# Three of five f32 table products moved from VectorE's queue to GpSimd's

## The chip, the cores and the metric

The kernel runs on one core of a Trainium2 chip. The metric is the device time of one execution in microseconds, and the time shown for the kernel before is the median of three runs: 236.66 us (236.27 to 236.88). The engines are named as in the profile: PE is TensorE, DVE is VectorE, ACT is ScalarE, POOL is GpSimd, SP is SyncE, which issues most of the DMAs. Each engine works through its own list of instructions in order; an instruction that waits for a semaphore holds up everything behind it on that engine.

## The reference

Two independent computations are set side by side in the output. The first is a linear attention over 2048 tokens and 16 heads of 28; the second is a long convolution of 2048 steps, with one kernel per channel that comes from a diagonal state space of 256 states for each of 448 channels.

```python
def _A_ref(x, wqkv, w_phi, wo):
    q, k, v = ...                                  # x @ wqkv, by heads
    phi_q = concat([softmax(q @ w_phi), softmax(-q @ w_phi)])
    phi_k = concat([softmax(k @ w_phi), softmax(-k @ w_phi)])
    kv = einsum("bhsf,bhsd->bhfd", phi_k, v); z = einsum("bhsf->bhf", phi_k)
    o = (phi_q @ kv) / (phi_q @ z + 1e-6)
    return o.reshape(B, S, D) @ wo

def _B_ref(u, A_re, A_im, B_re, B_im, C_re, C_im, log_dt, Dskip):
    dt = exp(log_dt)
    P = exp(dt * (A_re + 1j * A_im) * l)           # l = 0 .. 2047, rounded to bf16
    K = einsum("dn,dnl,dn->dl", C, P, dt * B).real
    y = irfft(rfft(u, padded) * rfft(K, padded))[:2048]
    return y + u * Dskip

return concat([_A_ref(...), _B_ref(...)], axis=-1)
```

## The kernel before

The exponentials P are not computed for each of the 2048 steps. Positions are written as sums of a few powers, and for each power k in `LOWP` = (128, 16, 8, 32, 64) (L344) a table `PW[k]` of the k-th power of every state's pole is made: a magnitude `amp[k]` (an exponential on ACT, f32, 896 columns), a cosine and a sine `cs[k]` (two activations on ACT, f32, 2 x 896 columns), and their product `PW[k]` (128 x 1792, bf16; for k = 128 an f32 `q128` that is squared for k = 256). The five products are the `mul` of L368, which goes through the helper `tt` (L177) and so runs on DVE:

```python
for k in LOWP:
    af(by_states(cs[k][:, 0, :]), from_states(bT), ACT.Sin, scale=float(k), bias=bias_hp)
    ...
    mul(PW[k] if k != 128 else q128, cs[k], amp[k].unsqueeze(1).to_broadcast([128, 2, NCOL]))
```

After that the kernel works on four groups of 112 channels. `tables(qt)` builds the two factor tables of group qt: `hi_tables` multiplies a start table step by step with `PW[16]`, `PW[32]`, `PW[64]` and `PW[128]` into `U_`, and `damp` and `far` build `W` from `PW[8]` and `PW[256]`. Both are chains of bf16 products and sums on DVE, with a few copies and squares on ACT. `build_k` contracts the two on PE. `signal_spectrum` transforms the input u on PE, and ACT copies each result out of PSUM into a tile `sg` (L419, L429), from where a DMA stores it. `key_side` and `query_side` are the attention; `kernel_spectrum` and `conv` are the spectral product and the inverse transform.

Nothing is scheduled at run time or by a planner at build time. The functions only record operations, and three lists written out in the file decide the rest: `ORDER` (L827) is the order in which all 1008 recorded operations are issued, and so the order of each engine's own list; `PLACES` (L865) is the address of every SBUF tile in one large buffer; `PICKS` (L885) says for operations that ACT or DVE could do which one does them. Waits are then put in by the framework, from what overlaps in memory.

Tiles share addresses where `PLACES` lets them, and three such overlaps touch this change. `cs[16]` lies on the bytes of two `sg` tiles; `cs[64]` lies on the bytes of another `sg` tile; the last part of `U_` of group 1 lies on the start of `cs[32]`. So ACT's first copy into the first of these `sg` tiles has to wait until the product for k = 16 has read `cs[16]`, ACT's next copy (into the `sg` on `cs[64]`) until the product for k = 64 has read it, and the copy that starts `U_` of group 1 (L545) until the product for k = 32 has. In the list of ACT these are three copies (L205 in the profile), in that order; in the list of DVE the products come in the order 16, 64, 32, with a cast between 64 and 32 that belongs to `PW[256]` (L375).

The other operations of DVE near them are, in this order: a subtraction for `q256` (f32), the three products and the cast, then two bf16 sums of `signal_spectrum` (`ab`, L414), a scaling in `damp` (L496, L208 in the profile) and the first product of `damp` (128 x 3136). The two sums wait for ACT's copies of `ur` (L413), the scaling and the product for the exponentials of `dampings` (L479), which ACT makes in between the copies into `sg`.

Of the kernel before, what the change touches and what calls it, by code (L numbers as in the profile page):

```python
# [12 lines left out]
ALU = mybir.AluOpType  # L13
# [11 lines left out]
NCOL = 4 * QC  # L25
# [94 lines left out]
def kernel(  # L120
# [17 lines left out]
    nc = tc.nc  # L138
# [11 lines left out]
    prog = Prog()  # L150

    def sb(shape, dtype=BF16):
        off = prog.place()
        size = int(np.prod(shape[1:])) * (4 if dtype == F32 else 2)
        v = sbuf[0:shape[0], off // 2:(off + size) // 2]
        if dtype == F32:
            v = v.bitcast(F32)
        names = "abcdefg"[:len(shape) - 1]
        if len(names) > 1:
            v = v.rearrange(f"p ({' '.join(names)}) -> p {' '.join(names)}",  # L160
                            **{n: s for n, s in zip(names[1:], shape[2:])})
        return v
# [13 lines left out]
    def tt(o, a, b, op):  # L176
        prog.add("V", lambda: nc.vector.tensor_tensor(out=o, in0=a, in1=b, op=op))  # L177

    def mul(o, a, b):
        tt(o, a, b, ALU.mult)  # L180
# [16 lines left out]
    def af(o, a, fn, **kw):  # L197
        prog.add("A", lambda: nc.scalar.activation(o, a, fn, **kw))  # L198
# [5 lines left out]
    def copy(o, a):  # L204
        either(lambda: nc.scalar.copy(o, a), lambda: nc.vector.tensor_copy(o, a))  # L205
# [64 lines left out]
    def load_u(b):  # L270
# [5 lines left out]
        out=ldt.rearrange("p (u j) -> p u j", u=2),  # L276
# [4 lines left out]
        out=raw["Are"].rearrange("p (u j) n -> p u (j n)", u=2),  # L281
# [32 lines left out]
    def from_states(bs):  # L314
        return view(psum[:, bs[0], 0:1], [512 * (bs[1] - bs[0]), 2], [56, 8], [1, 56])

    def by_states(v):
        return view(v, [56, 2], [112, 8], [1, 56])
# [26 lines left out]
    PW = {k: sb([128, 2, NCOL]) for k in (8, 16, 32, 64, 128, 256)}  # L345
    amp = {k: sb([128, NCOL], F32) for k in LOWP}
    cs = {k: sb([128, 2, NCOL], F32) for k in LOWP}
    q128, q256 = (sb([128, 2, NCOL], F32) for _ in range(2))
# [16 lines left out]
    for k in LOWP:  # L365
        af(by_states(cs[k][:, 0, :]), from_states(bT), ACT.Sin, scale=float(k), bias=bias_hp)
        af(by_states(cs[k][:, 1, :]), from_states(bT), ACT.Sin, scale=float(-k if k == 8 else k))
        mul(PW[k] if k != 128 else q128, cs[k], amp[k].unsqueeze(1).to_broadcast([128, 2, NCOL]))  # L368
        if k == 128:
            copy(PW[128], q128)  # L370
    s2 = sb([128, 2, NCOL], F32)
# [544 lines left out]
```

## Time and profile before

| | |
|---|---|
| median of three runs | 236.66 us (236.27 to 236.88) |
| profiled execution, whole | 235.22 us |
| its span (first to last instruction) | 233.5 us |
| busy: DVE / PE / ACT / POOL | 216.8 / 208.1 / 183.9 / 4.6 us |
| granted TensorE clock | 1.00 |

In the profile, a row of the timeline gives the start in us, the duration in us, the engine, the line, the operation, and the shapes as partitions x elements. A row of the chain of waits gives start, duration and what the chain ran through in that time. L177, L205, L198 and L208 are helper lines (a two-operand DVE operation, a copy, an activation, a scaling), so that rows are told apart by shape, start and neighbour rather than by line.

### The profile page before, as it was taken

The numbers are of one execution on the slowest core, as the hardware profiler recorded it, in microseconds if no ns is written. First come the engines' busy times: TensorE is split into PE (matmuls) and PEld (weight loads), VectorE is DVE, ScalarE is ACT, GpSimd is POOL, SyncE is SP. The second block draws the span as 40 slices with busy tenths as digits, with TensorE's granted clock in tenths as the row PEclk, the third lists the DMA queues.
The fourth block names the chain that finished last, engine by engine and source line by source line (L and its number), as shares of the span: only waits on it lengthen the run. The fifth ranks groups of instructions, "written<-read, shape, count | busy, mean of one in ns | idle before, by whom it ended". The sixth has DMA issues, their size and how long they took to land.

```text
span 233.5 us, 7103 instructions
## 1 busy us (share of the span) xinstructions
PE 208.1 (89%) x3044; PEld 152.8 (65%) x3044; DVE 216.8 (93%) x267; ACT 183.9 (79%) x321; POOL 4.6 (2%) x20
## 2 busy tenths in 40 slices
PE   1173899998999999999987999999999999999994
PEld 1161446564557655589765678885579968689993
DVE  1799999999999999989999979999999999999980
ACT  3999999999999999999998998698328451355331
POOL 4000000000000100000000000000000000000000
PEclk9999999999999999999999999999999999999999
DMA  5999910499239999826865899872696890489643
GB/s 154 237 218 272 151 37 1 167 150 235 71 59 190 147 176 257 152 71 155 206 156 144 99 255 225 226 114 61 70 368 131 199 277 10 63 185 242 121 100 81
DMA packets 81640, 36.40 MB, mean 156 GB/s; under 512 B 65480, under 2 KB 79688, under 8 KB 81224
## 3 DMA queue, kind: packets, MB, share of 16 engines
q1 hardware_dynamic: 81368, 35.71, 73.3%
q8 instruction: 24, 0.39, 0.7%
q10 hardware_dynamic: 240, 0.23, 0.3%
q14 instruction: 8, 0.07, 0.1%
HBM read 19.44 MB, written 8.62 MB: 120 GB/s over the span
## 4 chain that ended last, share of the span: by engine, by line
PE 51%; ACT 17%; DVE 13%; DMA 5%; issue 3%; SPq 0%; ACTq 0%
PE psum L220 51%; DVE sbuf L177 11%; ACT sbuf L198 8%; ACT sbuf L205 7%; DMA sbuf<-sbuf 3%; DMA sbuf<-KTd 2%; ACT L198 1%; DVE sbuf L205 1%; DVE sbuf L194 0%; ACT sbuf L211 0%; SPq L240 0%; DVE sbuf L212 0%; ACT sbuf L208 0%; DVE sbuf L208 0%; PE psum L230 0%
## 5 line engine op out<-in xcount | busy, mean ns | idle before, releaser
L220 PE MATMUL psum<-sbuf 128*128 128x112 bf16 (+9 forms) x3000 | 206.2, 252 | 21.4 <-ACT sbuf L205 7.8
L177 DVE TENSOR_TENSOR sbuf<-sbuf 128x896 bf16<-128x896 bf16 (+11 forms) x222 | 197.3, 956 | 7.2 <-ACT sbuf L198 4.3
L220 PEld LDWEIGHTS <-sbuf 128*128 128x128 bf16 (+3 forms) x3000 | 150.1, 114 | 75.3 <-issue 18.2
L205 ACT CAST sbuf<-psum 128x448 bf16<-128x448 f32 (+4 forms) x129 | 79.7, 672 | 38.0 <-PE psum L220 37.3
L198 ACT ACTIVATE sbuf<-psum 128x448 bf16<-128x448 f32 (+4 forms) x110 | 65.5, 721 | 0.5 <-PE psum L220 0.4
L211 ACT ACTIVATE sbuf<-sbuf 128x896 bf16<-128x896 bf16 x14 | 14.2, 1024 | 4.0 <-DVE sbuf L177 4.0
L198 ACT ACTIVATE sbuf<-psum,sbuf 128x896 f32<-128x896 f32 (+3 forms) x17 | 13.6, 835 | 0.0
L208 ACT ACTIVATE sbuf<-sbuf 128x896 bf16<-128x896 bf16 (+2 forms) x10 | 10.9, 1091 | 1.4 <-DVE sbuf L299 0.8
L198 ACT ACT_TABLE_LOAD x8 | 10.3, 1283 | 1.4 <-PEq L900 1.3
L205 ACT COPY sbuf<-sbuf 128x224 bf16<-128x224 bf16 (+2 forms) x18 | 8.9, 512 | 0.0
L205 DVE CAST sbuf<-psum 128x448 bf16<-128x448 f32 (+3 forms) x8 | 5.3, 690 | 2.3 <-PE psum L220 1.7
L215 POOL MEMSET sbuf<- 128x224 bf16 (+4 forms) x15 | 4.2, 314 | 153.3 <-PE psum L220 153.1
L205 ACT COPY sbuf<-psum 112x896 bf16<-112x896 bf16 (+2 forms) x13 | 6.8, 549 | 0.1
L177 DVE TENSOR_TENSOR sbuf<-psum,sbuf 128x448 bf16<-128x448 f32 (+3 forms) x12 | 5.1, 444 | 0.1
L194 DVE RECIPROCAL sbuf<-psum 128x64 bf16<-128x64 f32 x8 | 4.3, 546 | 0.4 <-ACT sbuf L198 0.3
L230 PEld LDWEIGHTS <-sbuf 112*112 112x112 bf16 (+1 forms) x44 | 3.1, 128 | 1.8 <-DVE sbuf L177 0.8
L230 PE MATMUL psum<-sbuf 112*112 112x112 bf16 (+1 forms) x44 | 3.6, 215 | 0.6 <-DVE sbuf L177 0.6
L212 DVE TENSOR_TENSOR sbuf<-sbuf 128x896 bf16<-128x896 bf16 (+1 forms) x3 | 3.3, 1087 | 0.0
L194 DVE RECIPROCAL sbuf<-sbuf 128x64 f32<-128x64 f32 x4 | 2.2, 545 | 0.0
L189 DVE SCALAR_TENSOR_TENSOR sbuf<-sbuf 128x64 f32<-128x64 f32 (+1 forms) x5 | 2.0, 393 | 0.0
L205 ACT CAST sbuf<-sbuf 128x1792 bf16<-128x1792 f32 x1 | 1.8, 1814 | 0.0
L208 DVE TENSOR_SCALAR sbuf<-sbuf 128x1568 bf16<-128x1568 bf16 (+1 forms) x3 | 1.6, 538 | 0.0
(8 smaller groups left out, 2.1 us busy)
## 6 DMA issues: line engine op xcount, KB each, us to landing
SUd<-sbuf SPq DMA_DIRECT2D x8, 448.0 KB
sbuf<-SCd SPq DMA_DIRECT2D x16, 224.0 KB
sbuf<-SUd SPq DMA_DIRECT2D x4, 896.0 KB
sbuf<-const SPq DMA_DIRECT2D x3, 1024.0 KB
sbuf<-const SPq DMA_DIRECT2D x8, 384.0 KB
sbuf<-in_B_u_dram SPq DMA_DIRECT2D x4, 448.0 KB
out_dram<-sbuf SPq DMA_DIRECT2D x4, 448.0 KB
out_dram<-sbuf SPq DMA_DIRECT2D x16, 112.0 KB
```

The lines of the kernel that those rows point to most:

```text
L177: prog.add("V", lambda: nc.vector.tensor_tensor(out=o, in0=a, in1=b, op=op))
L189: prog.add("V", lambda: nc.vector.scalar_tensor_tensor(out=o, in0=a, scalar=s, in1=b, op0=op0, op1=op1))
L194: nc.vector.reciprocal(o, a)
L198: prog.add("A", lambda: nc.scalar.activation(o, a, fn, **kw))
L205: either(lambda: nc.scalar.copy(o, a), lambda: nc.vector.tensor_copy(o, a))
L208: either(lambda: nc.scalar.activation(o, a, ACT.Copy, scale=s), lambda: nc.vector.tensor_scalar_mul(o, a, s))
L211: either(lambda: nc.scalar.activation(o, a, ACT.Square), lambda: nc.vector.tensor_tensor(out=o, in0=a, in1=a, op=ALU.mult))
L212: lambda: nc.vector.tensor_tensor(out=o, in0=a, in1=a, op=ALU.mult))
L215: prog.add("G", lambda: nc.gpsimd.memset(o, v))
L220: nc.tensor.matmul(o, lhsT=l, rhs=r, **kw)
L230: nc.tensor.transpose(o, i, idn)
```

## The change

In the kernel after, the products for k = 16, 32 and 64 are recorded for GpSimd and issued as its `tensor_tensor`, with the same operands and data types; those for k = 128 and 8 stay on DVE. They are no longer recorded through `mul`, so their line in the profile is L369. `ORDER`, `PLACES` and `PICKS` are unchanged, and with them the position of the products in the order of issue.

```diff
     for k in LOWP:
         af(by_states(cs[k][:, 0, :]), from_states(bT), ACT.Sin, scale=float(k), bias=bias_hp)
         af(by_states(cs[k][:, 1, :]), from_states(bT), ACT.Sin, scale=float(-k if k == 8 else k))
-        mul(PW[k] if k != 128 else q128, cs[k], amp[k].unsqueeze(1).to_broadcast([128, 2, NCOL]))
+        on_pool = k in (16, 32, 64)
+        prog.add("G" if on_pool else "V", lambda k=k, e=nc.gpsimd if on_pool else nc.vector: e.tensor_tensor(
+            out=PW[k] if k != 128 else q128, in0=cs[k], in1=amp[k].unsqueeze(1).to_broadcast([128, 2, NCOL]), op=ALU.mult))
         if k == 128:
             copy(PW[128], q128)
```

In the engines' lists this takes three rows out of DVE's and puts three next to each other into POOL's, in the order 16, 64, 32, behind five memsets and ahead of a 64 x 448 memset for a weight tile. The first of them waits for the cosine of k = 16 (ACT) and for what lay in its output's place before; the other two have their inputs by then. The three copies on ACT that waited for DVE's products now wait for POOL's: the one into the `sg` on `cs[16]` for the first product, the one into the `sg` on `cs[64]` for the second, the one that starts `U_` of group 1 for the third. On DVE one later subtraction of `hi_tables` waits for POOL's third product. All other waits that change on PE and SP are for POOL's later memsets and for DMAs that are issued tens of microseconds on.

## The prediction

> **What bounds the kernel now.** I read the busy times first, then the busy time by stretch of the span, then the chain of waits, then the timelines of DVE and ACT around the products.
>
> ```profile
> span 233.5 us, 7103 instructions
> PE 208.1 (89%) x3044; PEld 152.8 (65%) x3044; DVE 216.8 (93%) x267; ACT 183.9 (79%) x321; POOL 4.6 (2%) x20
> ```
> ```profile
> 26.30:37.00 10.70, 9.75 (x50) 4.84 (x49) 10.70 (x10) 10.67 (x18) 0.00 (x0) 1.00 0.30 57
> 37.00:50.00 13.00, 12.84 (x98) 7.65 (x96) 13.00 (x20) 12.86 (x17) 0.00 (x0) 1.00 0.55 123
> 50.00:93.60 43.60, 41.45 (x483) 24.88 (x481) 43.02 (x51) 43.47 (x86) 1.07 (x4) 1.00 0.83 159
> 93.60:129.70 36.10, 32.43 (x601) 25.73 (x600) 35.09 (x62) 35.05 (x66) 0.51 (x2) 1.00 0.65 143
> 129.70:230.10 100.40, 100.36 (x1742) 81.30 (x1741) 95.38 (x107) 58.89 (x111) 0.51 (x2) 1.00 0.77 162
> ```
> The columns of the second fence are the stretch and its length, then the busy time of PE, weight loads, DVE, ACT and POOL. DVE has the most work and POOL almost none, which speaks for moving work. But by stretch three engines are full at once. Between 26.3 and 50 us DVE is busy for all of the time and ACT for all but 0.17 us; from 50 to 93.6 ACT has 0.13 us left; from 129.7 to 230.1 it is PE. Time taken off DVE alone in the second stretch is worth only what ACT can follow.
>
> ```profile
> 32.62 3.91 DVE sbuf L177 x3
> 36.52 0.53 DVE sbuf L208
> 37.05 4.42 DVE sbuf L177 x5
> ...
> 48.50 0.20 ACT sbuf L208
> ...
> 93.61 6.15 DMA sbuf<-sbuf
> ...
> 129.69 31.20 PE psum L220 x553
> ```
> The chain that ends last runs over DVE to 48.5 us, over ACT to 93.6, over a transposing DMA and PE, and from 129.7 on over PE alone. So a delay of DVE or ACT near 37 us has nothing behind it that would take it in: the later links depend on it one after the other, and what ACT could make up is 0.14 us in 37 to 50.
>
> **DVE loses three products.** Here is DVE before, row by row: a bf16 sum, the f32 subtraction, the products for k = 16 and 64, the cast, the product for k = 32, two bf16 sums of the input's spectrum, the scaling, the first product of `damp`.
>
> ```profile
> 25.56 1.09 DVE L177 TENSOR_TENSOR sbuf<-sbuf 128x1792 bf16<-128x1792 bf16 x1
> 26.56 1.08 DVE L177 TENSOR_TENSOR sbuf<-sbuf 128x896 f32<-128x896 f32 x1
> 27.56 2.02 DVE L177 TENSOR_TENSOR sbuf<-sbuf 128x1792 bf16<-128x1792 f32 x1
> 29.50 2.02 DVE L177 TENSOR_TENSOR sbuf<-sbuf 128x1792 bf16<-128x1792 f32 x1
> 31.43 1.18 DVE L205 CAST sbuf<-sbuf 128x1792 bf16<-128x1792 f32 x1
> 32.51 2.01 DVE L177 TENSOR_TENSOR sbuf<-sbuf 128x1792 bf16<-128x1792 f32 x1
> 34.44 1.08 DVE L177 TENSOR_TENSOR sbuf<-sbuf 128x1792 bf16<-128x1792 bf16 x1
> 35.44 1.08 DVE L177 TENSOR_TENSOR sbuf<-sbuf 128x1792 bf16<-128x1792 bf16 x1
> 36.44 0.61 DVE L208 TENSOR_SCALAR sbuf<-sbuf 128x1568 bf16<-128x1568 bf16 x1
> 36.98 1.77 DVE L177 TENSOR_TENSOR sbuf<-sbuf 128x3136 bf16<-128x3136 bf16 x1
> ```
> 2.02 + 2.02 + 2.01 = 6.05 us go. What is late next is ACT:
>
> ```profile
> 25.10 1.18 ACT L198 ACTIVATE sbuf<-psum,sbuf 128x896 f32<-128x896 f32 x1
> 29.53 0.92 ACT L205 CAST sbuf<-psum 128x896 bf16<-128x896 f32 x1
> 30.76 0.94 ACT L205 CAST sbuf<-psum 128x896 bf16<-128x896 f32 x1
> 31.80 0.96 ACT L205 CAST sbuf<-psum 128x896 bf16<-128x896 f32 x1
> 34.18 0.65 ACT L198 ACTIVATE sbuf<-psum 128x448 bf16<-128x448 f32 x1
> 35.40 1.05 ACT L198 ACTIVATE sbuf<-psum 128x896 bf16<-128x896 f32 x1
> 36.99 0.70 ACT L205 COPY sbuf<-sbuf 128x448 bf16<-128x448 bf16 x1
> ```
> The two sums need the copy of `ur` that ends at 29.53 + 0.92 = 30.45; the scaling needs the exponential that ends at 34.83; the 128 x 3136 product needs the one that ends at 35.40 + 1.05 = 36.45. DVE began that product at 36.98. So even free products would bring DVE forward by 36.98 - 36.45 = 0.53 us and no more; the other 5.5 us become idle time in front of ACT. And since ACT is full itself, of the 0.53 us only the 0.14 us of its own idle time in 37 to 50 can reach the end. The gain is at most 0.1 to 0.5 us.
>
> **POOL gains three products.** Their price is not in the trace, since POOL does no two-operand work before. The rows of POOL by shape and window, the two memset rows from the start and from 77 us on:
>
> ```profile
> L279 POOL TENSOR_SCALAR_AFFINE_SELECT sbuf<-sbuf 112x112 bf16<-112x112 bf16 x1 | 0.3, 281 | 0.1
> L215 POOL MEMSET sbuf<- 64x448 bf16 x2 | 0.9, 465 | 0.0
> L215 POOL MEMSET sbuf<- 128x128 bf16 x1 | 0.2, 198 | 0.0
> ...
> L215 POOL MEMSET sbuf<- 64x448 bf16 x1 | 0.5, 465 | 0.0
> ```
> A memset writes one stream: (465 - 198) / (448 - 128) = 0.834 ns per element beside 91 ns fixed. The affine select reads one and writes one: (281 - 91) / 112 = 1.70 ns per element. For 1792 elements that is 1792 x 1.70 + 91 = 3.13 us if a second operand is free, and 1792 x 3 x 0.834 + 91 = 4.57 us if it costs a third stream. Below, the price of one stream, 1.59 us, is a floor; above, 4.57 is my ceiling. The affine select is the nearest row, and a product does more than it, so I take the middle of the two, 3.85 us, an estimate. The Trainium skill, GPSIMD Engine Reference, section Performance versus the Vector engine, states 4497 ns for such an f32 operation over 2048 elements, which would be 3.94 us here, an estimate from that page; the sum below would grow by 0.3 us with it.
>
> **The waits that move with them.** The first product needs the cosine that ends at 26.28 and can start at about 26.3. On ACT the copy at 30.76 now waits for product one, the copy at 31.80 for product two, the one at 36.99 for product three, and each holds all of ACT's list behind it, the exponentials for DVE among it. With nothing else in the way: product one ends at 30.2 (in time), product two at 26.35 + 2 x 3.85 = 34.05, product three at 37.9. ACT's second copy is then 34.05 - 31.80 = 2.25 us late, and its third copy, due at 36.99 + 2.25 = 39.2, is not held further. The 128 x 3136 product starts at 36.45 + 2.25 = 38.7 instead of 36.98. Less the 0.14 us, that is 2.1 us at the end. POOL's memset of a weight tile, now behind the products, comes at 38 to 43 us instead of about 3; its first reader is a multiplication in the key side, after 57 us, so it costs nothing. The one wait of DVE for product three stands behind the 128 x 3136 product and is met by then. The DMAs whose waits name POOL now are issued later still.
>
> **Do the two engines work beside each other?** The second unknown is whether POOL's reading runs freely beside DVE.
>
> ```profile
> 77.40 2.79 DVE L177 TENSOR_TENSOR sbuf<-sbuf 128x3136 bf16<-128x3136 bf16 x2 [0.38 <-ACT sbuf L205]
> ```
> ```profile
> 77.49 1.07 POOL L215 MEMSET sbuf<- 128x224 bf16 x4 [74.32 <-PE psum L220]
> ```
> Beside a busy DVE POOL only ever writes here: the 64 x 448 memset takes 465 ns in that place as it does at the start, before DVE's first work. The affine select, the only row that reads, ran with DVE idle. So the trace bounds it from both sides: no cost (2.1 us, above), or full exclusion, in which DVE's operations with operands in SBUF and POOL's products take turns. Then this holds for the stretch from 26.56 to the scaling: three products, the f32 subtraction, the cast and two bf16 sums, one after the other, 3 x 3.85 + 1.08 + 1.18 + 2 x 1.08 = 16.0 us, so that the scaling starts at 42.5 instead of 36.44, 6.1 us late. If DVE goes first whenever it can, product one waits for the cast (28.7), product two ends at about 38.4, ACT's second copy is 6.6 us late and the 128 x 3136 product starts at 36.45 + 6.6 = 43.1: again 6.1 us. The order of turns hardly matters, since both engines' work must fit in before the same point. With 3.13 and 4.57 us per product it is 3.9 and 8.3 us.
>
> I take exclusion as the likelier: no row supports the free case, as POOL has never read beside DVE here, and both stream f32 operands from the same 128 partitions. That is a judgement, not a reading. The Trainium skill, SBUF — State Buffer, section Who interferes with whom, states it as a rule: a VectorE instruction with two SBUF inputs and a GpSimd instruction that reads SBUF hold each other off for the whole instruction. No run here shows it; by that rule the sum is the 6.1 us.
>
> **The sum.** 0 to 0.5 us gained, 6.1 us lost, net 6.1, as the gain is inside the serial sum already. Against the profiled execution that is 235.22 + 6.1 = 241.3 us. That execution was 1.44 us below the median of the runs, 236.66, and the forecast is for a median: 242.8 us.
>
> **The rivals.**
> - POOL runs freely beside DVE, and only ACT's wait for product two costs: 236.66 + 2.1 = 238.8 us (237.4 at 3.13 us per product, 240.3 at 4.57). For it: the memset row. Against it: a memset reads nothing.
> - Not slower: the products hide under ACT. The point from which this decides is the copy at 31.80: two products must end by then, so one may take (31.80 - 26.35) / 2 = 2.7 us, with no interference. DVE's own 2.02 us would do. Then the time is 236.66 less 0.1 to 0.5, about 236.4 us. Against it: at 1.70 ns per element the affine select gives 3.13 us.
> - Worse than the sum: products over 4.57 us each, or DVE's operations themselves stretched; beyond 245 us.
> - That the products stay on DVE is excluded by the lists of the engines: they lose and gain exactly these three rows.
>
> **How the numbers follow.** Exclusion 0.50, free running 0.33, not slower 0.12, worse 0.05. The predicted time is that of the first, 242.8 us. The range from 237.4 (free running with the cheapest product) to 245.0 (exclusion with the dearest) leaves out 0.12 and 0.05; the forecast's own range is 240.6 to 245.0. About 0.3%, 0.7 us, is what a measurement of this kernel can tell from no change: faster by more 0.02, within it 0.10, slower 0.88.
>
> **What would show it.** Right: POOL has three L369 rows between 26 and 43 us, at 3.1 to 4.6 us each when alone; ACT's idle time before L205 copies is released by POOL; DVE idles, or its rows there get longer, and the 128 x 3136 product begins near 43 us; from there the timeline is the old one, shifted. If the product begins near 38.7 with DVE's rows at their old durations, the engines ran freely. Wrong: products under 2.7 us, a DVE that runs past ACT, or a shift at 43 us that is gone by 130.

## The result

The kernel after takes 244.17 us (median of 4 runs, 243.16 to 244.84) against 236.47 us for the kernel before in the same comparison (4 runs, 234.77 to 236.88): the ratio is 1.034, with a 95% interval of 1.027 to 1.040. It is slower by 7.7 us. The profiled execution took 244.84 us, beside 235.22 us before. The ratios here and below compare fast runs with fast runs and leave slow ones out, so that a ratio need not be the quotient of the medians beside it.

From the page of the kernel after, the span, the busy times, the granted clock of TensorE by slices of 6.1 us (in tenths; 9 stands for full speed) and the group of the three products (busy time and mean ns of one, then the idle time ahead):

```profile
span 243.1 us, 7104 instructions
PE 212.5 (87%) x3044; PEld 154.9 (64%) x3044; DVE 222.5 (92%) x264; ACT 184.4 (76%) x321; POOL 18.3 (8%) x23
PEclk9999997699999999999998899999999999999999
...
L369 POOL TENSOR_TENSOR sbuf<-sbuf 128x1792 bf16<-128x1792 f32 x3 | 13.7, 4598 | 23.5 <-PE psum L220 23.5
```

DVE has three instructions fewer and is busy 222.5 us instead of 216.8: it lost 6.05 us of products and gained 5.7 us of busy time. POOL's three rows last 4.6 us in the mean; how much of that is work shows when the two engines are read side by side. The timelines of POOL and of DVE of the kernel after (start, duration), around the products:

```profile
26.26 4.11 POOL L369 TENSOR_TENSOR sbuf<-sbuf 128x1792 bf16<-128x1792 f32 x1 [23.50 <-PE psum L220]
30.33 4.82 POOL L369 TENSOR_TENSOR sbuf<-sbuf 128x1792 bf16<-128x1792 f32 x1
35.10 4.87 POOL L369 TENSOR_TENSOR sbuf<-sbuf 128x1792 bf16<-128x1792 f32 x1
```
```profile
25.45 1.08 DVE L177 TENSOR_TENSOR sbuf<-sbuf 128x1792 bf16<-128x1792 bf16 x1
26.45 4.86 DVE L177 TENSOR_TENSOR sbuf<-sbuf 128x896 f32<-128x896 f32 x1
31.35 4.83 DVE L205 CAST sbuf<-sbuf 128x1792 bf16<-128x1792 f32 x1
36.07 4.85 DVE L177 TENSOR_TENSOR sbuf<-sbuf 128x1792 bf16<-128x1792 bf16 x1
40.84 1.08 DVE L177 TENSOR_TENSOR sbuf<-sbuf 128x1792 bf16<-128x1792 bf16 x1
41.84 0.61 DVE L208 TENSOR_SCALAR sbuf<-sbuf 128x1568 bf16<-128x1568 bf16 x1
42.38 1.77 DVE L177 TENSOR_TENSOR sbuf<-sbuf 128x3136 bf16<-128x3136 bf16 x1
```

The subtraction takes 4.86 us instead of 1.08, the cast 4.83 instead of 1.18, the first bf16 sum 4.85 instead of 1.08; the second sum, issued when POOL has ended, takes 1.08 as before. Read the ends of the rows, since a held instruction counts as busy: the sum of DVE ends at 26.53, product one at 30.37 (3.84 later), the subtraction at 31.31 (0.94), product two at 35.15 (3.84), the cast at 36.18 (1.03), product three at 39.97 (3.79), the first sum at 40.92 (0.95). One engine works at a time, and they alternate strictly. The scaling starts at 41.84 instead of 36.44, 5.4 us late.

ACT and PE behind it, in the timelines of the kernel after:

```profile
35.18 0.91 ACT L205 CAST sbuf<-psum 128x896 bf16<-128x896 f32 x1 [3.33 <-POOL sbuf L369]
42.00 0.56 ACT L205 COPY sbuf<-sbuf 128x448 bf16<-128x448 bf16 x1 [1.43 <-issue]
```
```profile
40.98 3.17 PE L220 MATMUL psum<-sbuf 128*128 128x448 bf16 x8 [3.17 <-DVE sbuf L177]
43.94 1.70 PE L230 MATMUL psum<-sbuf 112*112 112x112 bf16 x16
```
```profile
40.00:46.00 6.00, 5.03 (x26) 3.05 (x27) 6.00 (x6) 2.99 (x4) 0.38 (x1) 0.51 0.01 1
```

ACT's copy waits 3.33 us for product two. PE waits 3.17 us for DVE's first bf16 sum, and from then on its granted clock is 0.51 (the last fence: PE, weight loads, DVE, ACT, POOL, clock, DMA share and GB/s in 40 to 46 us): the 7 and the 6 in the slices of the page. The chain of waits of the kernel after has PE in it here, and is otherwise the old one, later:

```profile
31.35 0.06 DVE sbuf L205
...
36.07 4.86 DVE sbuf L177
...
40.98 3.17 PE psum L220 x8
...
101.23 6.15 DMA sbuf<-sbuf
...
139.33 31.18 PE psum L220 x534
```

The transposing DMA at 93.61 us before stands at 101.23, 7.62 us later; the last long link, on PE, at 139.33 instead of 129.69, 9.64 us later. So of the 9.62 us between the two profiled executions 7.6 are there by 101 us and 2.0 are added later. Lining up ACT's instructions one by one against those of the kernel before puts the 2.0 between 122.8 and 126.7 us of before, where PE waits for a DMA. This group before, and after:

```profile
124.21 1.43 PE L220 MATMUL psum<-sbuf 128*128 128x112 bf16 x20 [1.47 <-DMA sbuf<-KTd]
```
```profile
132.21 2.58 PE L220 MATMUL psum<-sbuf 128*128 128x112 bf16 x20 [1.84 <-DMA sbuf<-KTd]
```

Before, this group waited 1.47 us and took 1.43 us, at a clock of 1.00. Now it waits 1.84 and runs at about half the clock: 0.37 + 1.15 = 1.5 us of the 2.0.

### The profile page after: what moved, and what is told of

It is laid out like the page before. It is cut to its first block, busy times and chain, and to the rows that moved or that the text cites. A ratio compares the mean times of both kernels' runs of the same rounds, so it can differ in the third digit from the quotient of the medians.

```text
span 243.1 us, 7104 instructions
## 1 busy us (share of the span) xinstructions
PE 212.5 (87%) x3044; PEld 154.9 (64%) x3044; DVE 222.5 (92%) x264; ACT 184.4 (76%) x321; POOL 18.3 (8%) x23
## 4 chain that ended last, share of the span: by engine, by line
PE 52%; DVE 17%; ACT 10%; DMA 6%; issue 4%; SPq 0%; ACTq 0%
PE psum L220 51%; DVE sbuf L177 16%; ACT sbuf L205 5%; ACT sbuf L198 3%; DMA sbuf<-sbuf 3%; DMA sbuf<-KTd 2%; DMA SCd<-sbuf 1%; ACT L198 1%; PE psum L230 1%; ACT sbuf L211 1%; ACT sbuf L208 1%; DVE sbuf L194 0%; DVE sbuf L212 0%; SPq L240 0%; DVE sbuf L208 0%
## 5 line engine op out<-in xcount | busy, mean ns | idle before, releaser
L220 PE MATMUL psum<-sbuf 128*128 128x112 bf16 (+9 forms) x3000 | 210.2, 254 | 26.6 <-ACT sbuf L205 10.0
L198 ACT ACTIVATE sbuf<-psum 128x448 bf16<-128x448 f32 (+4 forms) x110 | 64.8, 705 | 1.0 <-PE psum L220 0.9
L369 POOL TENSOR_TENSOR sbuf<-sbuf 128x1792 bf16<-128x1792 f32 x3 | 13.7, 4598 | 23.5 <-PE psum L220 23.5
L230 PEld LDWEIGHTS <-sbuf 112*112 112x112 bf16 (+1 forms) x44 | 3.9, 159 | 2.1 <-DVE sbuf L177 0.8
L230 PE MATMUL psum<-sbuf 112*112 112x112 bf16 (+1 forms) x44 | 4.4, 248 | 0.6 <-DVE sbuf L177 0.6
L205 DVE CAST sbuf<-sbuf 128x1792 bf16<-128x1792 f32 x1 | 4.8, 4827 | 0.0
L369 DVE TENSOR_TENSOR sbuf<-sbuf 128x1792 f32<-128x1792 f32 (+1 forms) x2 | 4.0, 2024 | 0.1
```

What stands on the lines that cost most here:

```text
L220: nc.tensor.matmul(o, lhsT=l, rhs=r, **kw)
L230: nc.tensor.transpose(o, i, idn)
L369: prog.add("G" if on_pool else "V", lambda k=k, e=nc.gpsimd if on_pool else nc.vector: e.tensor_tensor(out=PW[k] if k != 128 else q128, in ...
```

## The experiments

Three questions were open: whether it is turns at SBUF that make the rows long; whether the fall of the clock is a second part of the cost; and whether the 2 us near 126 us belong to the change. In each result below, "at 57 us" is how much later than in the kernel before the activation of ACT that stood at 57.18 us starts, and so what the stage of the products costs by then; "behind 130 us" is the same for the one at 130.02. Both are read from one profiled execution.

**One product on POOL, and two.**

```diff
-        on_pool = k in (16, 32, 64)
+        on_pool = k == 16
...
+        on_pool = k in (16, 64)
```

> Only the product for k = 16 on POOL, those for 64 and 32 back on DVE. If the two engines take turns, the f32 subtraction on DVE is held again (about 4.9 us instead of 1.08), but nothing after it: the work that must fit in from 26.5 us on is one product of 3.85 us, two of 2.02 and the four DVE rows (4.25 us), so that the scaling comes at about 38.4 us, 1.9 us late, PE's gap before 41 us stays short, its clock stays at 1.00, and the time is about 238.3 us (ratio 1.008). If POOL's product ran freely and the long DVE rows came from something else, ACT's first copy at 30.7 us isn't held by a product that ends at 30.2, DVE waits for ACT as before, and the time is that of before, 236.3 us (ratio 0.999).

> The products for k = 16 and 64 on POOL, that for 32 on DVE. Taking turns: subtraction and cast held to about 4.8 us each, the two sums not; the scaling at about 40.2 us, 3.7 us late, and 240.2 us in all (ratio 1.016) if PE's clock stays at 1.00, up to 242 if it falls as in the changed kernel. If the loss of the changed kernel came from ACT's wait for product two alone, this run loses as much as with three products: 244 us (ratio 1.033).

With one: 238.16 us (10 runs) against 237.62 (23 runs), ratio 1.003 (0.998 to 1.008). With two: 240.71 us (4 runs), ratio 1.022 (1.014 to 1.029). Timelines of DVE, first with one product, then with two:

```profile
26.54 4.87 DVE L177 TENSOR_TENSOR sbuf<-sbuf 128x896 f32<-128x896 f32 x1
31.33 2.01 DVE L369 TENSOR_TENSOR sbuf<-sbuf 128x1792 bf16<-128x1792 f32 x1
38.27 0.61 DVE L208 TENSOR_SCALAR sbuf<-sbuf 128x1568 bf16<-128x1568 bf16 x1
```
```profile
26.51 1.09 DVE L177 TENSOR_TENSOR sbuf<-sbuf 128x896 f32<-128x896 f32 x1
27.64 4.85 DVE L205 CAST sbuf<-sbuf 128x1792 bf16<-128x1792 f32 x1
32.38 5.78 DVE L369 TENSOR_TENSOR sbuf<-sbuf 128x1792 bf16<-128x1792 f32 x1
40.09 0.61 DVE L208 TENSOR_SCALAR sbuf<-sbuf 128x1568 bf16<-128x1568 bf16 x1
```

With one product only the subtraction is held, and the next row is 2.01 us as before; the scaling is 1.83 us late. With two it is 3.65 us late, with three 5.4. Each product costs 3.8 us on POOL and saves DVE 2.0: 1.8 us net, three times over. In the second run the subtraction got in first (1.09 us) and product one was held instead; the sum up to the scaling came out the same. Behind the scaling the order did matter there. Product two ended later than with three products (36.27 us against 35.15), ACT's copy waited for it, and the 128 x 3136 product on DVE then waited 0.24 us for ACT:

```profile
36.31 0.91 ACT L205 CAST sbuf<-psum 128x896 bf16<-128x896 f32 x1 [3.67 <-POOL sbuf L369]
```
```profile
40.93 1.79 DVE L177 TENSOR_TENSOR sbuf<-sbuf 128x3136 bf16<-128x3136 bf16 x1 [0.24 <-ACT sbuf L198]
```

At 57 us the two runs are 1.8 and 4.2 us late, so the second loses 0.5 us more than its turns. How much of it is this wait is not separated. The total of the first is not told apart from no change: behind 130 us its profile shows 4.2 us, and the kernel before itself spread from 234.0 to 240.5 us here.

**POOL writes instead of reading.** Three memsets stand in the place of each product.

```diff
-        prog.add("G" if on_pool else "V", lambda k=k, e=nc.gpsimd if on_pool else nc.vector: e.tensor_tensor(
-            out=PW[k] if k != 128 else q128, in0=cs[k], in1=amp[k].unsqueeze(1).to_broadcast([128, 2, NCOL]), op=ALU.mult))
+        if on_pool:
+            prog.add("G", lambda k=k: [nc.gpsimd.memset(PW[k], 1.0) for _ in range(3)])
+        else:
+            mul(PW[k] if k != 128 else q128, cs[k], amp[k].unsqueeze(1).to_broadcast([128, 2, NCOL]))
```

> The three tables are not computed: POOL fills each with a constant by three memsets, some 14 us of writing (nine times 1.6 us) from about 25 us on, and reads nothing. DVE's list is that of the changed kernel. If what the engines share is the way by which POOL and DVE's second operand are read, the f32 subtraction and the two bf16 sums stay at 1.08 us beside the memsets; the cast, which has one operand but twice the subtraction's rate (1792 elements in 1.18 us against 896 in 1.08), shows whether a fast one-operand row is held by writes too, by up to one memset. ACT's copies don't wait for POOL, and the time is that of before, within 1 us. If any work of POOL holds DVE, the subtraction and the sums take 2 to 2.6 us each in this stretch.

234.97 us (2 runs), ratio 0.989 (0.980 to 0.998). Timeline of DVE:

```profile
26.51 1.09 DVE L177 TENSOR_TENSOR sbuf<-sbuf 128x896 f32<-128x896 f32 x1
27.64 2.05 DVE L205 CAST sbuf<-sbuf 128x1792 bf16<-128x1792 f32 x1
30.44 1.09 DVE L177 TENSOR_TENSOR sbuf<-sbuf 128x1792 bf16<-128x1792 bf16 x1 [0.76 <-ACT sbuf L205]
34.81 1.71 DVE L208 TENSOR_SCALAR sbuf<-sbuf 128x1568 bf16<-128x1568 bf16 x1 [2.28 <-ACT sbuf L198]
```

Beside a writing POOL, which was busy from 23.77 us for 15.8 us, the subtraction and the sums keep their 1.09 us; so writing does not hold them. The cast (1.18 before) and the scaling (0.61 before) are held by writing too, for 0.9 and 1.1 us. And the run prices the gain: with all three products off DVE and its two-operand rows free, DVE idles 0.76 and 2.28 us in front of ACT, and at 57 us the kernel is 0.34 us early.

**POOL reads one operand.** A copy of `cs[k]` into `PW[k]` stands in the place of each product; the diff is against the run with memsets.

```diff
-            prog.add("G", lambda k=k: [nc.gpsimd.memset(PW[k], 1.0) for _ in range(3)])
+            prog.add("G", lambda k=k: nc.gpsimd.tensor_copy(PW[k], cs[k]))
```

> The three products are replaced by plain copies of the cosine and sine table on POOL (the magnitudes are left out): one operand read instead of two, the same writes and the same waits on ACT. If the price goes by streams, a copy takes 3.1 us by the affine select's row, or 1.6 us if reading and writing overlap as in a memset's rate. If one read operand is enough to hold DVE, subtraction, cast and the first sum are each as long as one copy and their own 1.0 us, 2.6 to 4.1 us. If it needs both of POOL's operands, they stay at 1.08 and 1.18.

238.51 us (8 runs), ratio 1.006 (1.001 to 1.011). Timelines of POOL and of DVE:

```profile
26.36 6.89 POOL L370 CAST sbuf<-sbuf 128x1792 bf16<-128x1792 f32 x3 [23.60 <-ACT sbuf L198]
```
```profile
26.57 2.57 DVE L177 TENSOR_TENSOR sbuf<-sbuf 128x896 f32<-128x896 f32 x1
29.17 2.53 DVE L205 CAST sbuf<-sbuf 128x1792 bf16<-128x1792 f32 x1
31.61 2.57 DVE L177 TENSOR_TENSOR sbuf<-sbuf 128x1792 bf16<-128x1792 bf16 x1
```

The subtraction is held as soon as POOL reads one operand, so reading is what holds it: 2.57 us is its own 1.0 and a copy of about 1.55. That copy is a price that the trace of before did not have: 0.87 ns per element. The stage costs nothing here: at 57 us this run is 0.28 us early. Three copies and the held rows fit where three DVE products were, since a copy takes less than the 2.0 us that each saves. In the profiled execution 2.2 us are lost between 57 and 130 us (-0.28 there, +1.90 here), at 124 to 128 us above all, where the clock is 0.63; whether the 0.6% of the total is that in every execution is not shown.

**DVE reads PSUM beside the products.** The real part of q256 is left out; a copy from PSUM stands in the subtraction's place. In the first run it copies from the bank that the sines and cosines are made from, in the second from one that ACT no longer needs.

```diff
-    sub(q256[:, 0, :], s2[:, 0, :], s2[:, 1, :])
+    prog.add("V", lambda: nc.vector.tensor_copy(q256[:, 0, :].rearrange("p (k x) -> p k x", k=2), two(bT)))
...
+    prog.add("V", lambda: nc.vector.tensor_copy(
+        q256[:, 0, :].rearrange("p (k x) -> p k x", k=2), psum[:, b_, 0:D_MODEL].unsqueeze(1).to_broadcast([128, 2, D_MODEL])))
```

> The changed kernel with DVE's f32 subtraction left out and a copy of the same 896 f32 columns from PSUM in its place (q256's real part is then wrong): a DVE row that reads nothing from SBUF, next to POOL's first product. If the shared thing is the reading of SBUF, this row takes its 1.08 us while product one runs, product one takes 3.85 us from its start without a turn for DVE, and the cast behind it is the first row to be held. If a product of POOL holds all of DVE, this row takes 4.9 us as the subtraction did.

> As the run before with a PSUM copy in place of DVE's f32 subtraction, but from a PSUM bank that ACT is done with, so that the cosine is not held and product one starts at 26.3 us again; the copy comes at 26.5, beside it. If only reading SBUF is shared, the copy takes about 1.1 us inside product one, product one takes 3.85 us, and the cast behind the copy is held until product one has ended, about 30.2 us. If a product of POOL holds all of DVE, the copy takes 4.9 us.

The first, 245.13 us (2 runs), ratio 1.032 (1.022 to 1.041), did not answer the question: the copy held up ACT's cosine for 2.31 us, and product one, which needs the cosine, only began at 28.74 us, 1.1 us after the copy had ended. It does price a product on its own, since DVE had nothing to do from 28.82 to 32.86 us and product one took 3.96 us:

```profile
28.74 3.96 POOL L369 TENSOR_TENSOR sbuf<-sbuf 128x1792 bf16<-128x1792 f32 x1 [25.98 <-ACT sbuf L198]
```

The second took 241.24 us (2 runs), ratio 1.019 (1.008 to 1.031). Product one in its timeline of POOL, and its timeline of DVE:

```profile
26.32 4.11 POOL L369 TENSOR_TENSOR sbuf<-sbuf 128x1792 bf16<-128x1792 f32 x1 [23.57 <-DMA sbuf<-const]
```
```profile
26.52 1.08 DVE L375 COPY sbuf<-psum 128x896 f32<-128x896 f32 x1
27.64 3.84 DVE L205 CAST sbuf<-sbuf 128x1792 bf16<-128x1792 f32 x1
31.38 4.86 DVE L177 TENSOR_TENSOR sbuf<-sbuf 128x1792 bf16<-128x1792 bf16 x1
40.95 0.61 DVE L208 TENSOR_SCALAR sbuf<-sbuf 128x1568 bf16<-128x1568 bf16 x1
```

Product one ran from 26.32 us, and inside it the copy took 1.08 us. The next row, with its operand in SBUF, is held to the product's end at 30.43 us and takes its own 1.05 us from there. The scaling comes 0.9 us earlier than in the kernel after: one DVE row less in the turns. So a product on POOL does not hold all of DVE: a row that reads nothing from SBUF goes on beside it, though it writes there.

**The clock.** Matmuls that feed nothing fill the gap of PE in the kernel after, ahead of the group that waits 3.17 us. There are 40 of them in the first run; 50 in an earlier gap and 95 here in the second; 85 here alone in the third. The fourth is the kernel after, unchanged.

```diff
+    def fill(n, bank=0):
+        return [(psum[:, bank, 448:512], ident, REV[:, 0:64], dict(start=True, stop=True)) for _ in range(n)]
...
+                    if (b, k, mp) == (1, 3, 1):
+                        items = fill(40) + items
                     mms(items)
```

> The changed kernel with 40 small multiplications (128 x 64, into unused PSUM columns, read by nobody) on PE ahead of the multiplication that waits at 38 to 41 us. In the changed kernel the shift against before is 5.4 us at the scaling (41.84 against 36.44) but 7.7 at ACT's square (54.27 against 46.56), with PE's granted clock at 0.5 from 40 to 46 us and ACT waiting for PE. If the clock makes this difference, it stays at 1.00 here, the square comes at about 52.2 us and the time falls by 2 us to about 242.1 (ratio 1.024). If PE is merely late and the clock has no part, the time stays at 244.2 or gets worse by the added work (ratio 1.033 to 1.04).

> The changed kernel with more of the small multiplications: 50 in PE's gap before 36 us and 95 in the one before 41 us (1.6 and 3.0 us at the 32 ns each that the 40 took). With 40 the granted clock still fell, later and for a shorter time, and ACT's copy near 57 us was 6.3 us late instead of 7.5. If the clock is what adds to the 5.4 us of the scaling, it stays at 1.00 until 57 us here and that copy is 5.4 to 5.6 us late. If the work behind the gap is late for another reason, it stays at 6.3 or more.

> The changed kernel with 85 small multiplications (2.7 us) in PE's gap of 38 to 41 us alone; the 50 before 36 us are left out, since they had to wait for ACT and then ran at half the clock. If PE's granted clock makes the 2 us between the scaling (5.4 us late) and the copy near 57 us (7.5 late), the clock stays near 1.00 from 38 to 50 us and that copy is 5.4 to 5.7 us late. If not, it stays at 6.3 to 7.5.

> The changed kernel once more, beside the others. Both theories of the extra 2 us expect 241.5 to 245 us; its profile shows whether the clock's fall at 40 us comes each time (then the copy near 57 us is 7.5 us late again) or only in some executions (then 5.4).

With 40 of them: 246.12 us (4 runs), ratio 1.043 (1.036 to 1.050). They took 1.3 us, too little to close the gap, the clock still fell (0.62 in 42 to 46 us), and a second fall at 85 to 89 us cost more: no test. With 50 and 95: 245.25 us (4 runs), ratio 1.032 (1.021 to 1.044). The first 50 had to wait 3.47 us for ACT to free their PSUM bank, the clock fell behind that (0.50 in 38 to 41 us), and the filling, slowed by it, lasted until 46.8 us and made PE itself late: no test either. With 85 in the one gap: 243.29 us (2 runs), ratio 1.028 (1.016 to 1.040); the gap is 0.62 us, the clock is 1.00 from 34 to 54 us, and at 57 us the kernel is 5.30 us late instead of 7.46. This profile has a fall of its own, though: 0.50 from 18 to 24 us, ahead of everything that the filling touches and where the profiles of the kernels before and after have 1.00.

That looks like the answer, but the kernel after was run again, unchanged, in the same batch: 243.29 us (4 runs, 239.79 to 245.84), ratio 1.032 (1.022 to 1.041); by the medians, 243.29 and 237.45, the change costs 5.8 us in this batch and not 7.7. Its clock by slices, its timeline of PE, and its scaling on DVE:

```profile
PEclk9999999999999999999999999999999999999999
```
```profile
41.15 1.69 PE L220 MATMUL psum<-sbuf 128*128 128x448 bf16 x8 [3.17 <-DVE sbuf L177]
42.67 0.99 PE L230 MATMUL psum<-sbuf 112*112 112x112 bf16 x16
...
128.81 1.43 PE L220 MATMUL psum<-sbuf 128*128 128x112 bf16 x20 [0.40 <-DMA sbuf<-KTd]
```
```profile
42.02 0.61 DVE L208 TENSOR_SCALAR sbuf<-sbuf 128x1568 bf16<-128x1568 bf16 x1
```

The gap is the same 3.17 us, and the clock did not fall. So this program runs with the fall or without it, and the two profiles price it. Without it the scaling is 42.02 - 36.44 = 5.58 us late and nothing is added by 57 us, where it is 5.56; with it 5.40 became 7.46. At 57 us that is 7.46 - 5.56 = 1.9 us. The PE groups behind the gap are long enough for it: the first two take 3.17 - 1.69 and 1.70 - 0.99 longer, 2.2 us together, and part of the loss is made up by 57 us. But a filled gap without a fall proves nothing about filling, when an unfilled one has none either. What decides it in an execution stays open. With two products on POOL, PE's gap was 2.91 us, and the clock stayed at 1.00 as well.

**The late wait, in the kernel before.** Matmuls that feed nothing ahead of the group that waits for the DMA, 24 and then 60:

```diff
+                if (qt, m, b) == (0, 2, 0):
+                    items = fill(24, 7) + items
                 mms(items)
```

> The kernel before with 24 such small multiplications ahead of the multiplication that waits for a DMA at 122.7 to 124.2 us. The runs of the kernel before lie at 234.8 to 235.2 and at 236.3 to 236.9, and in the changed kernel's profile the same wait is followed by a granted clock of 0.57 for 4 us, which the profile of before doesn't have. If a clock that falls there in some executions makes the two sets, all runs here lie near 235.0 (ratio 0.994). If the sets have another cause, the median stays at 236.5 (ratio 1.000).

> The kernel before with 60 small multiplications (1.9 us) ahead of the multiplication that waits for a DMA near 122 to 124 us; 24 of them took 0.7 us and left 2.3 us of PE's wait open, after which the clock fell. If that fall costs 1 to 2 us in many executions, the median falls by about 1 us (ratio 0.995); where the DMA lands early the added work costs up to 0.5. If other gaps decide, nothing changes (ratio 1.00).

237.24 us (12 runs), ratio 1.007 (1.002 to 1.012), and 237.53 us (12 runs), ratio 1.004 (1.000 to 1.008). The profile of the first, with the product work as it was before, shows the late fall: PE waits 2.27 us there and the twenty matmuls take 2.59 us, at a clock of 0.50.

```profile
125.55 2.59 PE L220 MATMUL psum<-sbuf 128*128 128x112 bf16 x20 [2.27 <-DMA sbuf<-KTd]
```

With 60 the clock did not fall in the profiled execution, and no time was gained over the runs. So the late wait and the fall behind it also come without this change: the wait is 0.40 us in the one profile of the kernel after, 1.84 in the other, 1.47 before and 2.27 here. Between 57 and 130 us the kernel after makes up 1.0 us in the one profile and loses 2.2 in the other, and this run loses 2.9. Over all profiles in which PE waits there, the clock fell behind six of the seven waits of 1.84 to 2.56 us, and behind none of the five of 0.40 to 1.47; the one that it passed by is the longest, 2.56 us, with two products on POOL.

## Why the prediction was right

It said 242.8 us and slower, by exclusion; 244.17 us was measured. By its own steps:

- **What bounds the kernel, and that a delay near 37 us goes through to the end.** Right. The links of the chain follow each other at 93.6 and 129.7 us as before, later, and from 57 to 123 us the delay in the profile stays within 7.4 to 7.6 us.
- **DVE's 6.05 us are worth 0.1 to 0.5 us at most.** Right: with memsets on POOL the stage was 0.34 us early and DVE idled in front of ACT, as the times at which ACT's exponentials end said.
- **POOL's price, 3.85 us.** Right: 3.84, 3.84 and 3.79 us from end to end, and 3.96 us for one with nothing beside it. The figure of the Trainium skill, GPSIMD Engine Reference, section Performance versus the Vector engine, gave an estimate of 3.94 us; the trace agrees within 4%. How the price was reached was partly luck. The affine select, taken as the row for one read and one write at 1.70 ns per element, was no measure: a copy from f32 reads and writes at 0.87. The step from a copy to a product of two operands is what is dear, (3.84 - 1.55) / 1792 = 1.3 ns per element, and the middle between two wrong ends fell on the sum.
- **Exclusion, called a judgement.** Right, and now shown by runs: two-operand rows of DVE stretch by a whole product beside POOL's reads (4.86 us) and not beside its writes (1.09), and a copy from PSUM is not held (1.08). This is the rule of the Trainium skill, SBUF — State Buffer, section Who interferes with whom, also in its finer point: the cast and the scaling, with one operand each, were held by writes as well (2.05 and 1.71 us), as the Trainium skill states there for DVE's two-port modes, which casts and scalings can enter; that these two rows ran in such a mode is not shown.
- **The sum, 6.1 us for the stage.** 5.4 measured at the scaling. The term that was too large is DVE's: its four rows between and behind the products were counted at their durations, 1.08 + 1.18 + 2 x 1.08 = 4.42 us, and took 0.94 + 1.03 + 0.95 + 0.92 = 3.84 us from end to end, since each row overlaps the one before. The timeline of before shows that: rows of 1.08 us start 1.00 us apart.
- **What waits next.** One wait was overlooked. ACT's copy at 42.00 us, the start of `U_`, stands in the prediction as waiting for product three; product three ended at 39.97, but DVE's two sums ended at 41.92, and the copy started then. The profile names no releaser for this wait; in the run with the second PSUM copy, too, this copy starts right behind the second sum (41.10 and 41.03 us). ACT is 42.00 - 36.99 = 5.0 us late there, less than DVE's 5.4, so that it changed nothing in the sum.
- **What is missing: the clock.** The prediction had PE's matmuls at an unchanged clock. The stall leaves PE without work for 3.17 us, and in the first profile the granted clock then fell to half for 6 us: 1.9 us more at 57 us. The execution without a fall was 5.56 us late there, the one with it 7.46. How often it falls is not known from two profiles. That the fall follows from the gap is argued from its place, and not shown, since the same gap did not always bring it. The Trainium skill, TensorE: Matmul & The Clock Gate, section HAM oscillation — how this bites in real kernels, has a threshold of about 3.4 us of idle time; here the clock fell behind 3.17 us in one execution and stayed in the other, and it fell behind six shorter waits, of 1.84 to 2.52 us, near 126 us. The Trainium skill's same page also has the window over which activity is counted run freely against the program (section What's actually happening), which would fit two outcomes of one gap; no run here tests it.

The forecast fell 1.4 us short of the median. It had 0.7 us too much for the turns and 0.2 us too much in its median of before, and nothing for the remaining 7.7 - 5.4 = 2.3 us, of which a fall of the clock behind the stall is worth 1.9; the late wait, which the sum also left out, differs by 3.2 us between the two profiles of the kernel after. That the number came so near is in part luck: a term that was too large stood against a cost that was left out, and the later batch of the same two kernels, with 5.8 us between the medians, lies on the other side of the predicted 6.1. What the runs bear out is the mechanism, by the 1.8 us for each product.

The rival of free running is out, by the rows at 4.86 us; the one that was not slower as well, since a product takes 3.8 us against the 2.7 that it needed.

## What to carry to other kernels

Before moving work to GpSimd to relieve VectorE, ask what VectorE does beside it: if both read SBUF and VectorE's instructions there have two operands, the work does not run beside but in turns, and a product that takes 2.0 us on VectorE and 3.8 on GpSimd costs the difference. Read such a case by the ends of the rows, since time held is shown as busy time of VectorE and not as a wait; an engine whose instructions go down and whose busy time does not is the sign. And when a stall reaches TensorE, price the clock as well, but by several profiles of the same program.

## What the runs showed of the hardware

- With both engines ready, one product on POOL and one DVE row alternate: no run shows two products in a row while DVE had a row waiting. At the start either can get in first: with two products on POOL, the subtraction went ahead of product one, whose row starts 0.19 us before it.
- On POOL, for 1792 elements on 128 partitions, f32 to bf16: 3.8 to 4.0 us for a product of two operands, about 1.55 us for a copy.
- The granted clock fell to 0.50 to 0.51 behind a gap of 3.17 us in one execution and stayed at 1.00 behind the same gap, in the same program, in another.
- The same unchanged kernel spread over 6.5 us here (234.0 to 240.5 us for the kernel before in 23 runs), where the three runs shown first had agreed within 0.6 us. With that, effects under 1% needed the profile by stage, and not the total, to be seen.
